# A new instruction order and bank table for attention plus MLP on one core, with the last output block in halves

## The chip, the cores and the metric

The kernel runs on one core of one Trainium2 chip. The metric is the device time of one execution in microseconds (us); lower is better. TensorE's granted clock is listed with each run, as a share of full speed. Engine names as in the profile: PE is TensorE (matmuls), PEld its weight loads, DVE is VectorE, ACT is ScalarE, POOL is GpSimd, SP is SyncE; an SPq or ACTq row, or a POOL row with DMA_DIRECT2D, is a transfer being issued by that engine.

## The reference

Random-feature attention on 8 batches of 8 heads, 576 rows of 64, followed by a two-layer MLP with a sigmoid gate. Inputs and output are float32; the kernel multiplies in bf16.

```python
def _attn_ref(q, k, v, omega):
    m, D = omega.shape                       # 128, 64
    scale = 1.0 / np.sqrt(np.sqrt(D))
    def phi(x):
        proj = np.einsum('bhsd,md->bhsm', x, omega)
        h = proj - np.sum(x * x, axis=-1, keepdims=True) / 2.0
        h = h - np.max(h, axis=-1, keepdims=True)
        return np.exp(h) / np.sqrt(m)
    q_p, k_p = phi(q * scale), phi(k * scale)
    kv = np.einsum('bhsm,bhsd->bhmd', k_p, v)
    z = np.sum(k_p, axis=2)
    num = np.einsum('bhsm,bhmd->bhsd', q_p, kv)
    den = np.einsum('bhsm,bhm->bhs', q_p, z)[..., None] + 1e-06
    return num / den
# x: the attention, 4608 rows of 512
def _moe_ref(x, w_in, w_out):                # 512 -> 2048 -> 512
    h = x @ w_in
    return (h * (1.0 / (1.0 + np.exp(-1.702 * h)))) @ w_out
```

## The kernel before

The program first lists operations with their dependences, then places them on engines by written-out orders: `ORDER` has for each engine the numbers of its operations, `BANK` the PSUM bank of each group of matmuls (PSUM takes their results; the table has eight banks). The SP ring below is the row of transfers that SyncE issues, in its order. Both were found by a search over a cost table; on the chip each engine runs its list in order, and waits where an operation is not ready (in the trace of after VectorE stood idle for 1.56 us before a copy at 10.48 us, though the input of the reduction behind it in its list was ready at 9.6).

Of the kernel before, what the change touches and what calls it, by code (L numbers as in the profile page):

```python
# [7 lines left out]
ALU = mybir.AluOpType  # L8
# [6 lines left out]
PE = "pe"  # L15
# [3 lines left out]
SP = "sp"  # L19
# [10 lines left out]
BANKS = dict(b0="H0 H1 O0 O1 P0 P1 S0 S1", b1="O1 P0 P1 S0 S1", b2="O1 P0 P1 S0 S1", bv="H0 H1 P0 P1 S0 S1", H="H0 H1", O="O0 O1", Oend="O0 O1 P0 P1")  # L30
# [5 lines left out]
QL_SW = 2  # L36
# [13 lines left out]
    om=(30.0, 0.0, 400.0), qk=(45.0, 1200.0, 770.0), ql=(26.5, 600.0, 630.0), qlc=(26.5, 800.0, 770.0), vl=(26.0, 600.0, 640.0),  # L50
    v=(51.0, 1600.0, 700.0), vw=(51.0, 1200.0, 640.0), qkl=(45.0, 1000.0, 770.0), w=(78.0, 2000.0, 810.0), T=(25.3, 100.0, 1250.0), os=(90.0, 100.0, 620.0),
# [6 lines left out]
        88, 50, 10, 54, 52, 66, 57, 56, 90, 71, 65, 72, 93, 99, 92, 115, 120, 98, 119, 142, 78, 144, 147, 117,  # L58
        152, 80, 146, 153, 125, 105, 83, 126, 132, 110, 107, 86, 219, 134, 137, 159, 113, 221, 253, 164, 140,
        161, 251, 223, 217, 167, 231, 172, 277, 169, 255, 175, 275, 301, 299, 178, 241, 303, 246, 184, 243,  # L60
        181, 265, 249, 187, 267, 270, 193, 279, 273, 196, 202, 313, 383, 211, 315, 289, 318, 205, 291, 294,
        190, 389, 297, 214, 199, 390, 208, 321, 391, 338, 335, 392, 347, 356, 384, 341, 395, 396, 353, 344,
        397, 398, 365, 457, 401, 402, 362, 350, 417, 385, 371, 359, 409, 403, 404, 477, 380, 368, 427, 386,
        437, 377, 467, 432, 429, 556, 472, 487, 374, 469, 447, 492, 562, 489, 449, 563, 557, 452, 564, 558,
        559, 565, 610, 574, 575, 576, 577, 650, 514, 582, 511, 568, 508, 520, 630, 569, 529, 517, 570, 590,
        538, 526, 571, 620, 535, 523, 729, 622, 532, 625, 660, 640, 544, 600, 541, 665, 645, 662, 735, 553,
        605, 602, 730, 642, 547, 550, 736, 763, 737, 731, 732, 755, 687, 738, 684, 693, 741, 681, 783, 742,
        773, 743, 775, 702, 778, 696, 744, 803, 747, 748, 749, 750, 823, 690, 813, 705, 793, 818, 815, 699,
        795, 902, 708, 798, 833, 714, 838, 903, 835, 711, 723, 908, 720, 956, 717, 904, 909, 936, 726, 854,
        910, 860, 905, 863, 857, 928, 914, 866, 911, 869, 915, 946, 920, 966, 875, 971, 948, 916, 917, 976,  # L70
        921, 878, 951, 968, 872, 996, 922, 986, 881, 923, 1129, 890, 884, 991, 1075, 1006, 988, 1101, 899,
        1076, 1011, 1109, 893, 1008, 887, 1081, 1082, 896, 1169, 1083, 1077, 1084, 1078, 1093, 1149, 1094,
        1033, 1119, 1095, 1030, 1027, 1124, 1087, 1042, 1088, 1051, 1036, 1121, 1089, 1139, 1045, 1060, 1090,
        1282, 1039, 1096, 1141, 1144, 1048, 1159, 1274, 1054, 1302, 1248, 1057, 1179, 1161, 1063, 1292, 1164,
        1066, 1181, 1184, 1294, 1249, 1072, 1069, 1322, 1260, 1297, 1250, 1261, 1342, 1251, 1203, 1206, 1266,
        1332, 1267, 1352, 1215, 1212, 1334, 1312, 1262, 1337, 1357, 1263, 1224, 1354, 1221, 1254, 1233, 1314,
        1200, 1255, 1317, 1209, 1218, 1256, 1227, 1257, 1236, 1242, 1427, 1245, 1364, 1428, 1373, 1230, 1268,
        1382, 1239, 1429, 1361, 1269, 1370, 1391, 1415, 1379, 1400, 1416, 1388, 1417, 1397, 1406, 1418, 1367,
        1409, 1410, 1487, 1411, 1376, 1481, 1385, 1394, 1412, 1403, 1482, 1421, 1483, 1433, 1436, 1422, 1442,
        1484, 1445, 1423, 1454, 1451, 1424, 1460, 1488, 1489, 1463, 1439, 1490, 1448, 1430, 1457, 1512, 1505,  # L80
        1466, 1499, 1500, 1501, 1469, 1502, 1526, 1478, 1527, 1506, 1493, 1507, 1475, 1513, 1472, 1494, 1495,
        1514, 1508, 1515, 1496, 1519, 1520, 1521, 1522, 1528, 1529,
    ],
    ACT: [
        51, 89, 9, 60, 61, 59, 70, 73, 75, 74, 101, 68, 102, 95, 100, 97, 122, 124, 129, 154, 151, 156, 127,
        155, 128, 133, 149, 220, 87, 160, 114, 141, 226, 218, 225, 236, 237, 235, 227, 173, 238, 233, 170, 260,
        261, 257, 176, 259, 179, 242, 262, 308, 309, 185, 305, 182, 266, 250, 307, 188, 310, 194, 285, 284,
        197, 286, 203, 283, 281, 212, 206, 191, 215, 200, 209, 339, 336, 393, 348, 357, 342, 345, 354, 399,
        366, 463, 459, 461, 462, 363, 351, 422, 464, 419, 423, 421, 360, 424, 412, 413, 411, 372, 405, 482,
        483, 381, 481, 484, 369, 479, 387, 442, 443, 441, 439, 444, 378, 375, 560, 616, 615, 566, 617, 612,  # L90
        614, 578, 655, 656, 652, 515, 512, 584, 585, 654, 509, 521, 586, 636, 657, 632, 530, 635, 518, 595,
        634, 539, 597, 527, 637, 592, 572, 536, 524, 596, 594, 533, 545, 542, 554, 548, 551, 768, 769, 765,
        733, 688, 770, 759, 757, 685, 758, 767, 739, 694, 788, 682, 787, 789, 790, 703, 785, 697, 808, 745,
        805, 809, 807, 810, 751, 829, 828, 691, 825, 827, 706, 830, 700, 709, 715, 712, 724, 721, 961, 958,
        962, 960, 718, 941, 727, 963, 938, 943, 855, 861, 940, 942, 906, 864, 858, 932, 930, 912, 931, 870,
        867, 876, 918, 982, 981, 983, 980, 978, 879, 873, 1001, 1002, 998, 1000, 1003, 882, 924, 1135, 1133,
        891, 1134, 1131, 885, 1104, 1103, 1136, 900, 1105, 1115, 1114, 894, 1111, 1113, 888, 897, 1173, 1174,
        1171, 1116, 1085, 1175, 1176, 1155, 1153, 1151, 1034, 1079, 1031, 1028, 1043, 1154, 1156, 1052, 1037,
        1046, 1061, 1091, 1288, 1287, 1040, 1284, 1097, 1286, 1049, 1277, 1278, 1289, 1055, 1308, 1276, 1304,
        1058, 1307, 1306, 1064, 1067, 1073, 1070, 1328, 1327, 1326, 1324, 1309, 1348, 1252, 1329, 1344, 1347,  # L100
        1349, 1204, 1346, 1207, 1216, 1213, 1264, 1225, 1222, 1234, 1201, 1210, 1219, 1228, 1258, 1237, 1243,
        1246, 1365, 1374, 1231, 1383, 1240, 1362, 1270, 1371, 1392, 1380, 1401, 1389, 1398, 1419, 1407, 1368,
        1377, 1386, 1395, 1413, 1404, 1434, 1437, 1443, 1485, 1446, 1455, 1452, 1425, 1461, 1464, 1440, 1491,
        1431, 1449, 1458, 1467, 1470, 1479, 1503, 1476, 1473, 1509, 1516, 1497, 1523, 1530,
    ],
    DVE: [
        4, 5, 8, 19, 14, 2, 11, 3, 12, 6, 55, 53, 58, 69, 91, 13, 67, 96, 116, 94, 121, 143, 123, 79, 145, 150,
        118, 148, 81, 106, 84, 85, 82, 108, 111, 109, 112, 138, 135, 139, 136, 222, 254, 165, 162, 163, 252,
        166, 224, 168, 234, 232, 278, 174, 256, 258, 171, 276, 302, 300, 177, 180, 304, 247, 248, 244, 245,
        186, 306, 183, 268, 269, 271, 272, 189, 195, 280, 282, 198, 314, 204, 274, 290, 213, 316, 317, 292,  # L110
        295, 296, 293, 207, 319, 192, 320, 216, 298, 201, 322, 210, 340, 337, 349, 358, 343, 346, 355, 460,
        458, 367, 364, 418, 352, 420, 410, 361, 373, 480, 478, 382, 428, 370, 440, 438, 468, 430, 433, 431,
        473, 474, 488, 434, 448, 470, 493, 471, 490, 450, 451, 376, 379, 453, 491, 454, 494, 613, 611, 651,
        653, 583, 516, 513, 510, 631, 522, 633, 531, 519, 591, 593, 540, 528, 621, 537, 525, 623, 626, 627,
        534, 661, 624, 641, 546, 601, 666, 646, 663, 647, 667, 664, 606, 543, 555, 643, 644, 607, 603, 604,
        552, 764, 549, 756, 766, 689, 686, 695, 786, 774, 683, 776, 784, 779, 777, 780, 704, 804, 698, 806,
        826, 824, 814, 692, 794, 819, 820, 707, 816, 817, 796, 797, 701, 799, 800, 834, 710, 716, 836, 839,
        840, 837, 713, 725, 957, 959, 722, 719, 939, 937, 728, 856, 862, 865, 859, 929, 871, 868, 947, 967,
        949, 972, 950, 973, 877, 979, 977, 952, 953, 969, 970, 874, 997, 999, 987, 880, 883, 1132, 1130, 992,
# [225 lines left out]
def bass_performer_favor__then__act_gelu_quick_kernel(  # L345
# [136 lines left out]

    def load_ql(b, key, ckey, after=()):
        s = b % 2
        pool = b >= QL_SW
        if b in LWB:
            for nm, t, c in (("k", kd, 1), ("q", qd, 0)):
                dst = bass.AP((QL if pool else QLF)[s], 256 * c, [[512, 128], [1, 256]])
# [620 lines left out]
```

## Time and profile before

| | before |
|---|---|
| time, median of 3 runs | 324.75 us (324.12 to 325.43) |
| TensorE busy | 307.4 us, 96% of the profiled span |
| VectorE, ScalarE, GpSimd busy | 190.7, 187.3, 113.1 us |
| first matmul | 5.7 us after the start |
| after the last matmul | 4.0 us |

The matmuls all belong to one engine that is busy in nearly all of the span, so the kernel is TensorE-bound and an order can win only where TensorE waits or runs at half clock (until 12.08 us by the trace's clock records; four 128-column transposes take 0.61 us at 8.14 and 0.39 at 12.96): at the start, at the end, and in rare gaps between. The prediction shows the lines and reads them.

### The profile page before, as it was taken

To read this page: it belongs to the slowest core of one execution; us is meant where nothing else is said; L and a number is where in the kernel's file an instruction comes from. 1 tells how busy PE (TensorE), PEld (TensorE's weight loads), DVE (VectorE), ACT (ScalarE), POOL (GpSimd) and SP (SyncE) were. 2 spreads that over 40 slices of the span, in tenths; PEclk is the share of its full clock that TensorE was granted. 3 is DMA by queue.
4 is the path that set the end of the run, shared out by engine and by line. 5 is a ranking of instruction groups with operands and counts; after the bars stand their busy time and mean duration, and the time that the engine had idled before them with its cause. 6 is when DMAs were issued, how large, how long until landed. Compare 5 with 4: busy or idle time off the path is not lost.

```text
span 321.7 us, 5787 instructions
## 1 busy us (share of the span) xinstructions
PE 307.4 (96%) x2246; PEld 151.2 (47%) x2246; DVE 190.7 (59%) x401; ACT 187.3 (58%) x378; POOL 113.1 (35%) x185
## 2 busy tenths in 40 slices
PE   1798999999999999999999999999999999999994
PEld 1574554445544544454454544454544444444442
DVE  0899985368656784686648745788574533342210
ACT  1789855489178646665658766686545543343231
POOL 6696283627019705933644364031200000000000
PEclk9999999999999999999999999999999999999999
DMA  7999999996889989998999999933022002011005
GB/s 134 241 226 222 207 210 222 151 145 129 209 163 206 226 120 162 245 193 155 141 159 194 207 158 168 151 99 61 2 41 86 0 2 98 33 67 65 33 17 148
DMA packets 84119, 44.20 MB, mean 137 GB/s; under 512 B 54844, under 2 KB 77756, under 8 KB 84092
## 3 DMA queue, kind: packets, MB, share of 16 engines
q0 software_dynamic: 29792, 20.45, 42.0%
q1 hardware_dynamic: 54300, 23.37, 35.4%
q8 instruction: 18, 0.29, 0.4%
q14 instruction: 9, 0.07, 0.1%
HBM read 36.73 MB, written 9.44 MB: 144 GB/s over the span
## 4 chain that ended last, share of the span: by engine, by line
PE 86%; ACT 5%; DVE 5%; DMA 2%; issue 1%; POOL 1%; POOLq 0%
PE HT L427 36%; PE OB L427 34%; PE PB L427 11%; PE SB L427 4%; ACT QKP L641 3%; DMA QK<-in_q_dram 2%; DVE GT L966 1%; DVE NM L631 1%; ACT TH L961 1%; DVE OO L855 1%; ACT QKL L641 1%; POOL QK L478 1%; DVE TT L598 0%; DVE RD L847 0%; PE PB L868 0%
## 5 line engine op out<-in xcount | busy, mean ns | idle before, releaser
L966 DVE SCALAR_TENSOR_TENSOR GT<-TH,HT 128x512 bf16<-128x512 f32 x144 | 97.8, 683 | 80.4 <-ACT TH L961 80.0
L427 PE MATMUL HT<-XT,WIN 128*128 128x512 bf16 x576 | 142.2, 379 | 0.6 <-DVE GT L966 0.3
L961 ACT ACTIVATE TH<-HT 128x512 f32<-128x512 f32 x144 | 86.2, 600 | 82.7 <-PE HT L427 74.9
L427 PE MATMUL OB<-WOUT,GT 128*128 128x512 bf16 x496 | 122.5, 379 | 0.0
L427 PEld LDWEIGHTS HT<-XT,WIN 128*128 128x128 bf16 x576 | 52.7, 98 | 61.5 <-DVE GT L966 7.7
L427 PEld LDWEIGHTS OB<-WOUT,GT 128*128 128x128 bf16 x496 | 45.7, 98 | 53.4 <-issue 3.4
L780 POOL TENSOR_TENSOR VP<-VS,WW 128x512 bf16<-128x512 f32 x32 | 33.5, 1050 | 38.8 <-ACT WW L774 38.7
L641 ACT ACTIVATE QKP<-PB 128x512 bf16<-128x512 f32 x54 | 31.4, 600 | 7.2 <-PE PB L427 4.1
L641 ACT ACTIVATE QKP<-SB 128x512 bf16<-128x512 f32 x56 | 33.0, 606 | 2.8 <-PE SB L427 1.1
L995 ACT ACTIVATE OS<-OB 128x512 f32<-128x512 f32 x31 | 18.6, 599 | 16.7 <-PE OB L427 16.6
L631 DVE TENSOR_REDUCE NM<-SB 128x4 f32<-128x512 f32 x31 | 20.9, 682 | 8.8 <-PE PB L427 7.4
L631 DVE TENSOR_REDUCE NM<-PB 128x4 f32<-128x512 f32 x23 | 15.5, 683 | 6.9 <-PE PB L427 5.3
L427 PE MATMUL PB<-WOUT,GT 128*128 128x512 bf16 x80 | 19.4, 379 | 0.0
L478 POOL DMA_DIRECT2D QK<-in_k_dram x17 | 13.4, 790 | 7.1 <-DMA QK<-in_q_dram 4.2
L789 POOL CAST VP<-WW 128x8 bf16<-128x8 f32 x32 | 7.0, 225 | 24.3 <-ACT WW L774 24.3
L855 DVE TENSOR_TENSOR OO<-PB,RD 128x320 bf16<-128x320 f32 x29 | 13.7, 485 | 0.4
L478 POOL DMA_DIRECT2D QK<-in_q_dram x17 | 13.0, 768 | 0.0
L503 POOL DMA_DIRECT2D QL<-in_k_dram x12 | 7.8, 649 | 13.6 <-DMA TT<-QK 13.6
L427 PEld LDWEIGHTS PB<-WOUT,GT 128*128 128x128 bf16 x80 | 7.8, 98 | 9.5 <-DVE GT L966 0.3
L855 DVE TENSOR_TENSOR OO<-SB,RD 128x320 bf16<-128x320 f32 x24 | 11.5, 482 | 0.3
L532 POOL DMA_DIRECT2D VS<-in_v_dram x12 | 7.8, 661 | 7.2 <-DMA TT<-QK 7.2
L427 PE MATMUL PB<-TT,omB 64*128 64x512 bf16 (+1 forms) x31 | 10.2, 377 | 0.0
(140 smaller groups left out, 285.7 us busy)
## 6 DMA issues: line engine op xcount, KB each, us to landing
out_dram<-OS SPq DMA_DIRECT2D x32, 256.0 KB, 2.8
VS<-in_v_dram POOLq DMA_DIRECT2D x12, 512.0 KB, 6.6
QK<-in_k_dram POOLq DMA_DIRECT2D x15, 256.0 KB, 6.4
QK<-in_q_dram POOLq DMA_DIRECT2D x15, 256.0 KB, 7.3
WIN<-in_moe_w_in_dram POOLq DMA_DIRECT2D x4, 512.0 KB, 10.7
WOUT<-in_moe_w_out_dram POOLq DMA_DIRECT2D x4, 512.0 KB, 17.2
VS<-in_v_dram SPq DMA_DIRECT2D x4, 256.0 KB, 6.4
VS<-in_v_dram SPq DMA_DIRECT2D x2, 512.0 KB, 12.4
```

What stands on the lines that cost most here:

```text
L427: return lambda e: e.matmul(o() if callable(o) else o, lhsT=l, rhs=r, **kw)
L478: POOL, lambda e, dst=dst, so=so: e.dma_start(dst, so), 800, key,
L503: POOL if pool else SP, lambda e, dst=dst, so=so: e.dma_start(dst, so), 120, key,
L532: SP if b < V_SW else POOL, lambda e, dst=dst, so=so: e.dma_start(dst, so), 120, key,
L631: lambda e: e.tensor_reduce(out=o, in_=bass.AP(TILE[gr.bank], 0, [[512, 128], [128, 4], [1, 128]]), axis=AX.X, op=ALU.max, negate=True,),
L641: lambda e: e.activation(out=o, in_=view(gr, 0, pat or [[1, 512]])(), func=ACTF.Exp, scale=scale),
L780: lambda e: e.tensor_tensor(out=VP[vs][:, :, 0:64], in0=bass.AP(V, t * 9 * 64 + 64, [[NT * 9 * 64, 128], [64, 8], [1, 64]]), in1=bass.AP(W ...
L789: POOL, lambda e: e.tensor_copy(out=VP[vs][:, :, 64], in_=WW[vs][:, :]), 140, key + K_W + 240,
L855: lambda e, gr=gr, x=x: e.tensor_tensor(out=OO[os_][:, 5 * x : 5 * x + 5, :], in0=bass.AP(TILE[gr.bank], 0, [[512, 128], [65, 5], [1, 64]] ...
L961: lambda e, gr=gr, th=th: e.activation(out=TH[th][:, :], in_=at(gr, 0, 512)(), func=ACTF.Tanh, scale=0.851),
L966: lambda e, gr=gr, th=th, jc=jc: e.scalar_tensor_tensor(out=GT[gi][:, jc, :], in0=TH[th][:, :], scalar=1.0, in1=at(gr, 0, 512)(), op0=ALU. ...
L995: lambda e, gr=gr, os_=os_: e.activation(out=OS[os_][:, :], in_=at(gr, 0, 512)(), func=ACTF.Copy, scale=0.5),
```

## The change

A wider search: all kinds of PSUM groups but one (`bv`, not printed below) may take any of the eight banks, costs of some loads are raised, orders and banks come out new on all five engines, and the last output block is split so that less work follows the last matmul.

```diff
-BANKS = dict(b0="H0 H1 O0 O1 P0 P1 S0 S1", b1="O1 P0 P1 S0 S1", ..., H="H0 H1", O="O0 O1", Oend="O0 O1 P0 P1")
+BANKS = dict(b0="H0 H1 O0 O1 P0 P1 S0 S1", b1="H0 H1 O0 O1 P0 P1 S0 S1", ..., Oend="H0 H1 O0 O1 P0 P1 S0 S1")
-QL_SW = 2
+QL_SP = (0, 1)
+TAIL = True
 ...                                     # DMA_KIND: two fixed costs 1200 and 1000 -> 1300
     SP: [                               # the other engines' orders are new as well
-        18, 17, 20, 7, 22, 21, 28, 27, 46, 48, 42, 47, ...
-        802, 782, 822, 734, 746, 781, 740, 752, 955, 821, 926, 801, 975, 841, 927, 995, ...
+        22, 18, 7, 17, 47, 20, 48, 21, 28, 27, 46, 45, ...
+        573, 567, 579, 926, 734, 781, 955, 740, 752, 975, 746, 821, 801, 841, 927, 995, ...
 ...                                     # BANK: a new table
+    def last_block(gi, key):            # the last 128 rows, two halves of 256 columns
+        for half in range(2):
+            ...                         # 4 x 4 matmuls of 256 columns into one bank
+            cut = 128 if half else 256
+            ...                         # ScalarE evacuates columns 0 to cut
+            if half:
+                ...                     # VectorE evacuates columns 128 to 256
+            for h in range(2):
+                g.add(ACT if half and h else SP, ... dma_start ...)
 ...
+            if TAIL and sbi == 8 and rb == 3:
+                last_block(gi, win2(9))
+                continue
```

In the SP order, 926, 955 and 975 are the transposes of pairs 0, 1 and 2 of batch 5, and 781, 821, 801 and 841 those of the finished attention of batch 4 into XT. Before, 975 stood between 801 and 841. Now it stands ahead of 821, 801 and 841.

## The prediction

> **What bounds the kernel now.** I read the page first, then busy times by stage, the waits of TensorE, the timelines of the first 16 us and the last 10 us, and then the starts of single matmuls. The page, engines and slices:
>
> ```profile
> span 321.7 us, 5787 instructions
> PE 307.4 (96%) x2246; PEld 151.2 (47%) x2246; DVE 190.7 (59%) x401; ACT 187.3 (58%) x378; POOL 113.1 (35%) x185
> PE   1798999999999999999999999999999999999994
> ```
>
> TensorE is the bound: it is idle only in the first six slices and the last. Busy times of four stages (columns: stretch, length, busy us of each engine, clock, DMA share, GB/s):
>
> ```profile
> 0.00:12.00 12.00, 5.03 (x36) 3.49 (x37) 3.63 (x15) 3.45 (x7) 6.42 (x14) 1.00 0.91 169
> 12.00:40.00 28.00, 25.36 (x322) 16.05 (x321) 25.81 (x63) 25.61 (x59) 19.40 (x32) 1.00 1.26 222
> 40.00:312.00 272.00, 271.31 (x1867) 129.28 (x1866) 161.22 (x325) 156.17 (x311) 87.31 (x140) 1.00 0.73 127
> 312.00:322.00 10.00, 5.71 (x27) 2.39 (x25) 0.00 (x0) 2.09 (x4) 0.00 (x0) 1.00 0.51 133
> ```
>
> From 12 to 40 us three engines are at 91 to 92% together: attention of batches 0 and 1 must be exponentiated and evacuated before the large matmuls exist that need neither ScalarE nor VectorE. From 40 to 312 us TensorE lacks 0.7 us in 272. A matmul's record overlaps the next, so a busy PE can hide waits; I therefore took the start-to-start distance of neighbouring matmuls minus 216 ns per 512 columns. That shows 5.67 us before the first matmul; about 5.9 us of loss to 16 us (waits and half-speed matmuls); about 4.4 us from 16 to 40; and 7 us from 40 to 312, of which some 6 are not waits: 35 projections on 64 rows cost about 0.1 us on entering and 0.1 on leaving. True waits after 40 us are only about 1.0 us, 0.7 of it one wait at 179.7. At the end 4 us follow the last matmul. So all that an order can win is about 5.7 + 5.9 + 2.8 (true waits, 16 to 40) + 1.0 + 4.0 = 19 us, most of it in latencies that stay. TensorE's waits:
>
> ```profile
> PE OB L725 <- DMA QK<-in_k_dram: 5.7, 1, 5.7
> PE SB L725 <- DMA QK<-in_k_dram: 0.9, 1, 0.9
> PE PB L427 <- ACT QKP L641: 0.7, 1, 0.7
> PE HT L427 <- DVE TT L598: 0.6, 1, 0.6
> PE HT L868 <- DVE OO L855: 0.6, 1, 0.6
> PE PB L427 <- ACT TH L961: 0.6, 1, 0.6
> ```
>
> No wait recurs: no wait for a PSUM bank is long enough to be a bound. The end, from the timeline:
>
> ```profile
> 312.37 5.34 PE L427 MATMUL PB<-WOUT,GT 128*128 128x512 bf16 x24
> 317.75 0.60 ACT L995 ACTIVATE OS<-PB 128x512 f32<-128x512 f32 x1 [1.13 <-PE PB L427]
> 318.37 1.11 SPq L1012 DMA_DIRECT2D out_dram<-OS  x2
> ```
>
> After the last matmul come one 0.60 us evacuation, two issues one after the other, and a landing.
>
> [...] four transposes take 0.61 us at 8.14 and 0.39 at 12.96. [...]
>
> **The change part by part.**
>
> Title items that change nothing: the leftover q/k rows of batches 0 and 1 were already on the SP ring with casts (the old threshold 2 selects the same batches). The new branches for split leftovers need a batch that is both at least 1 and in (0,), so they never run. Costs and descriptor counts only fed the search; the orders are written out. What is left is the order, the bank table, fourteen moved small operations and the last block.
>
> (1) Last block. 16 matmuls of 512 columns become 32 of 256: 32 x 109 = 3.49 us for 16 x 216 = 3.45, plus 0.04. The weight loads (98 ns each) fit under 109. The last half is evacuated by ScalarE (128 columns) and then VectorE (128 columns) from one bank, hence one after the other: from 0.60 us at 512 and 0.20 at 8 columns, ScalarE takes about 0.30; VectorE about 0.25; with two hand-overs of 0.06 this equals the old 0.60 plus 0.06, so no gain. The two stores are issued by two sequencers at once (saves 0.55) and carry 64 KB instead of 128 (I choose 0.25 less than the 2.4 us landing). Sum: about -0.7 us, all on the path.
>
> (2) Banks and order from 40 us on. The waits here sum to 1.0 us; the new order has 34 instead of 35 runs of 64-row projections (-0.2). I give it -0.3, since new small waits come in too.
>
> (3) Start. K of pair 0 is loaded first, then K and Q of pair 1, then K of pairs 2 and 3. On the SP ring a leftover load of batch 1, which is gated on pair 1's Q, is now fifth. The ring stops there with 640 packets issued, where by 15 us it formerly had moved 1,536. GpSimd's queue moved about 150 packets per us beside it and up to 380 when alone (10 to 11 us, counted in the trace), so batch 0's last Q should land near 12 us instead of 15.0. That is a gain for supply.
> Against it: TensorE's first instruction is now the omega transpose. Omega landed at 7.5 us; as third on its ring I estimate 6.5 to 7.5. Then follow in a row: cast 0.20, transpose 0.31, two copies and four memsets 0.8, the copy of pair 0's K 0.42, two cold projections 0.9, transposes of pair 1 (0.6), its copy 0.42, and only then the first reduction, which stands behind that copy in VectorE's order. That is near 11.3 instead of 10.58, and ScalarE's first exponential near 12.5 instead of 11.01. Afterwards the two engines should be fed better: between 12 and 40 us VectorE was idle 2.2 us and ScalarE 2.4 (28 minus 25.81 and 25.61), and a win of half, 1.2 us, is my choice. The fourteen moves are nearly even: five copies go from ScalarE to VectorE and six back, one cast goes each way between VectorE and GpSimd, and the identity memset leaves GpSimd. I set the sum of the start at -0.7 us: gains of 1.2 and of the earlier q/k (0.7), less 1.2 for the later first exponential.
>
> Sum: -0.7 - 0.3 - 0.7 = -1.7 us; 324.75 - 1.7 = 323.1.
>
> **Rivals.** (a) The start loses: exponentials begin 1.5 us later, TensorE is busy too little before 12 us [...]. For it: the order of waits above, and one omega load in front of all. Against: transposes, projections and late loads still fill 8 to 12 us. It would make +1 to +2 us at the start, 325 in all. (b) The start wins clearly: loads land 3 us earlier, 12 to 40 us has no waits (2.8 us) and the 4.2 us lost between 8 and 16 halve. For it: K first gives both engines work sooner, GpSimd's queue is freed. Against: 91% on two engines means that work, not supply, limits that stage. It makes -4 to -5 us: 320. (c) Early loads of batch 1 and the first weights wait behind GpSimd operations that now stand before them in its order (a copy of batch 0's first weights before Q of batch 1). For it: that copy can run at about 13 us, and this Q was issued at 11.56. Against: the queue held other work and landed it at 19.05, some 7 us after its issue. It would make under +1 us. (d) The middle gets worse: any bank may now delay the large matmuls behind a reduction or evacuation. At most a few waits of 0.5 us.
>
> **Range and chances.** The 0.7 us at the end is nearly certain to within 0.4; the start is uncertain to plus or minus 2 us, the middle to 0.7, the run-to-run spread 0.6. So 320.7 to 325.5. Faster by 2% needs under 318.3, a gain of 6.4 of the 19 us listed, most of them latencies: 0.05. Slower by 2%, over 331.2, needs a stall of 6 us that the search would have seen: 0.02.
>
> **What would show it.** End: last output issue on two sequencers together, under 3.2 us from last matmul to end of span. Start: batch 0's last Q landing near 12 us, omega's transpose first at about 7.3, the first exponential after 12, and VectorE and ScalarE over 93% busy from 13 to 38 us. Middle: TensorE lacking under 1 us between 40 and 312. The prediction is wrong if the matmuls stay slow after 12.1 us, if TensorE has a wait over 2 us past 16 us, or if 256-column matmuls start further apart than 109 ns.

## More of the kernel before

```python
# pair t (two heads) of batch b: its Q and K are transposed by the DMA; the landing is also "tgo"
g.add(SP, lambda e: e.dma_start_transpose(tout, tin), 150, key - 5000,
      reads=[("q", s, t), ("k", s, t)],
      writes=[("Tk", tt), ("Tq", tt), ("tgo", b, t)], dma=f"d_T{tt}", ...)
...
# the finished pair of attention is transposed into XT, the MLP's input:
#   OO -> XT, one transfer for each pair, ("xt", t, b) is written      (SP ring too)
...
def stage1(sbi):                       # x @ w_in for batch sbi
    rd = [("xt", t, sbi) for t in range(NT)]           # NT = 4: all four pairs
    ...                                # 16 chains of four 512-column matmuls,
                                       # tanh on ScalarE, product on VectorE -> GT
def stage2(sbi):                       # GT @ w_out, 4 blocks of 16 matmuls, ScalarE, store
...
for b in range(1, B):
    stage1(b - 1)
    if b >= 2:
        stage2(b - 2)
    attend(b)
    if b + 1 < B:
        gate = [("wout", 2)] if b == 1 else [("tgo", b, 2)]
        load_qk(b + 1, 0, 4, ..., after=gate)     # casting loads, issued by GpSimd
        load_qk(b + 1, 4, 4, ..., after=gate)
        load_ql(b + 1, ..., after=gate)
        load_v(b + 1, 0, NT, ..., after=gate)
```

The last lines matter most below: the loads of batch b + 1 are released when the transpose of pair 2 of batch b has landed, wherever that transpose stands in the SP ring's order.

## The result, and the profile after

The changed kernel took 328.61 us (median of 4 runs: 326.55, 328.47, 328.74, 328.87); the kernel before took 324.53 us (4 runs of the same rounds). The ratio is 1.0108, with a 95% interval of 1.0061 to 1.0154. It is the mean time of one kernel's fast runs over the mean of the other's of the same rounds, so not quite the ratio of the medians. Executions over 1.5% slower than the fastest of the same kernel are left out of the means. Within 2%, but 5.5 us above the predicted time and above the range.

From the page of the kernel after: span, engines (busy us, share, instructions), and two rows of the 40 slices, TensorE's busy tenths and its granted clock.

```profile
span 327.1 us, 5780 instructions
PE 306.4 (94%) x2224; PEld 154.2 (47%) x2262; DVE 189.3 (58%) x402; ACT 185.6 (57%) x380; POOL 113.0 (35%) x184
PE   1878999999999999999599999999999999999995
PEclk9999999999999999999699999999999999999999
```

Busy time is 1 us less and the span is 5.4 us more (327.1 against 321.7), so it is waiting. The twentieth slice (155 to 164 us) is half empty, and the clock falls in the same slice. (The trace lacks 38 matmul records, by its count of 2,262 weight loads, none of them in this stretch; I worked from the weight loads.) The same stages as in the prediction, and 150 to 170 us by itself:

```profile
0.00:12.00 12.00, 3.78 (x31) 3.14 (x32) 3.12 (x15) 2.08 (x3) 6.38 (x13) 1.00 0.98 149
12.00:40.00 28.00, 24.72 (x311) 16.53 (x311) 24.55 (x59) 25.95 (x59) 18.86 (x31) 1.00 1.24 220
40.00:312.00 272.00, 266.07 (x1821) 127.85 (x1852) 161.33 (x329) 154.54 (x313) 87.79 (x141) 0.99 0.72 127
150.00:170.00 20.00, 16.44 (x81) 6.71 (x81) 8.29 (x13) 10.79 (x25) 6.71 (x11) 0.83 1.41 175
```

TensorE's wait list of after, longest first (columns: engine, output bank, line, what ended the wait; total, times, longest):

```profile
PE SB L568 <- DVE om_raw L450: 7.2, 1, 7.2
PE PB L428 <- issue: 3.7, 2, 3.6
PE PB L428 <- ACT QKP L644: 1.7, 1, 1.7
```

The first is the start, as predicted. The second is new, a single wait of 3.6 us whose releaser the view does not see ("issue"). The timeline around it shows what was in flight. A row gives start, length, engine, line, operation, output <- input.

```profile
143.66 1.29 SPq L790 DMA_TRANSPOSE TT<-QK  x1
146.19 3.94 SPq L906 DMA_TRANSPOSE XT<-OO  x3
147.02 0.81 POOL L545 DMA_DIRECT2D VS<-in_v_dram  x1 [6.67 <-DMA TT<-QK]
147.82 0.77 POOL L479 DMA_DIRECT2D QK<-in_q_dram  x1
...
152.60 0.70 POOL L504 DMA_DIRECT2D QL<-in_k_dram  x1
159.50 1.48 PE L428 MATMUL PB<-XT,WIN 128*128 128x512 bf16 x3 [3.56 <-issue]
```

The transpose of pair 2 of batch 5 (143.66) now goes out before the last three XT transposes of batch 4. Its landing at 146.73 releases GpSimd at 147.02, and GpSimd issues nine loads of batch 6 until 153.3. Two of the XT transposes are then still to be issued (147.44 and 148.76). They land at 153.63 and 159.03. The first matmul of stage 1 of batch 4 reads all four pairs of XT and starts at 159.50. The same stretch of the kernel before:

```profile
142.18 1.20 SPq L878 DMA_TRANSPOSE XT<-OO  x1
...
144.78 1.29 SPq L878 DMA_TRANSPOSE XT<-OO  x1
146.17 1.25 SPq L762 DMA_TRANSPOSE TT<-QK  x1
147.47 1.29 SPq L878 DMA_TRANSPOSE XT<-OO  x1
...
149.71 0.62 POOL L532 DMA_DIRECT2D VS<-in_v_dram  x1 [7.17 <-DMA TT<-QK]
```

There the releasing transpose is issued at 146.17, one place before the last XT transpose, which lands at 150.24. The first load is issued at 149.71, too late to slow it by much (2.77 us from issue to landing). The margin was small, though: experiment 3 releases the loads one pair earlier in the order of before, and that does the same harm. The landing times by tile say it in one line each. Before, then after, over three XT transposes:

```profile
DMA to landing us min/median/max: 2.7/2.8/2.8
```

```profile
DMA to landing us min/median/max: 2.6/6.2/10.3
```

The stall is paid twice. TensorE stood idle from 155.94 to 159.50 (3.56 us), and the trace's clock records show half speed from 158.28 to 165.11, so the matmuls after the wait started 0.43 us apart instead of 0.216: 165.11 - 159.50 = 5.61 us at half speed are another 2.8 us. Together that is 6.4 us. The timed runs agree: of the four, the one whose clock stayed at 1.00 took 326.55 us, the two at 0.99 took 328.74 and 328.87.

To compare whole kernels I worked out "matmul time lost" for each trace: the time of a matmul's start minus the sum of what all earlier matmuls take back to back at full clock (64-row projections in pairs). It counts waits and half-speed alike. The unit is us:

| lost up to | before | after | difference |
|---|---|---|---|
| 20 us | 12.40 | 13.85 | +1.45 |
| 40 us | 15.97 | 17.28 | +1.31 |
| 150 us | 19.61 | 20.26 | +0.65 |
| 170 us | 20.08 | 27.08 | +7.00 |
| 312 us | 23.20 | 29.24 | +6.04 |
| end of the span | 27.76 | 33.06 | +5.30 |

So +1.3 came at the start, -0.7 from 40 to 150, +6.35 between 150 and 170 us, -1.0 in the rest of the middle, and -0.74 at the end. The end of after:

```profile
322.33 1.47 PE L428 MATMUL PB<-WOUT,GT 128*128 128x256 bf16 x12
323.84 0.28 ACT L1022 ACTIVATE OS<-PB 128x128 f32<-128x128 f32 x1 [0.93 <-PE PB L428]
324.14 0.29 DVE L1030 TENSOR_SCALAR OS<-PB 128x128 f32<-128x128 f32 x1 [12.62 <-ACT OS L1022]
324.47 0.55 ACTq L1040 DMA_DIRECT2D out_dram<-OS  x1
```

ScalarE and VectorE go one after the other (0.28 and 0.29 us), and the last store leaves on ScalarE's sequencer. From the last matmul's end to the end of the span: 3.28 us, before 4.03.

### The profile page after: what moved, and what is told of

It is laid out like the page before. It is cut to its first block, busy times and chain, and to the rows that moved or that the text cites.

```text
span 327.1 us, 5780 instructions
## 1 busy us (share of the span) xinstructions
PE 306.4 (94%) x2224; PEld 154.2 (47%) x2262; DVE 189.3 (58%) x402; ACT 185.6 (57%) x380; POOL 113.0 (35%) x184
## 4 chain that ended last, share of the span: by engine, by line
PE 87%; ACT 5%; DVE 2%; issue 2%; DMA 1%; SPq 0%; POOL 0%; POOLq 0%; ACTq 0%
PE OB L428 26%; PE HT L428 23%; PE SB L428 20%; PE PB L428 18%; ACT QKP L644 3%; DMA om_f<-in_omega_dram 1%; DVE GT L994 1%; ACT TH L989 1%; PE HT L753 0%; ACT TT L598 0%; ACT XT L598 0%; DVE OO L883 0%; DVE NM L632 0%; ACT QKL L644 0%; DVE TT L599 0%
## 5 line engine op out<-in xcount | busy, mean ns | idle before, releaser
L428 PE MATMUL OB<-WOUT,GT 128*128 128x512 bf16 x249 | 63.3, 383 | 0.6 <-issue 0.2
L428 PE MATMUL HT<-XT,WIN 128*128 128x512 bf16 x183 | 48.3, 385 | 0.4 <-issue 0.2
L994 DVE SCALAR_TENSOR_TENSOR GT<-TH,HT 128x512 bf16<-128x512 f32 x47 | 32.0, 682 | 22.3 <-ACT TH L989 22.1
L994 DVE SCALAR_TENSOR_TENSOR GT<-TH,SB 128x512 bf16<-128x512 f32 x41 | 27.9, 682 | 27.4 <-ACT TH L989 27.3
L989 ACT ACTIVATE TH<-HT 128x512 f32<-128x512 f32 x47 | 28.2, 603 | 26.9 <-PE HT L428 21.8
L428 PE MATMUL SB<-XT,WIN 128*128 128x512 bf16 x162 | 42.1, 382 | 0.8 <-ACT QKP L644 0.6
L428 PE MATMUL PB<-XT,WIN 128*128 128x512 bf16 x113 | 30.3, 386 | 3.8 <-issue 3.6
L428 PE MATMUL HT<-WOUT,GT 128*128 128x512 bf16 x109 | 27.6, 379 | 0.2
L428 PEld LDWEIGHTS HT<-XT,WIN 128*128 128x128 bf16 x188 | 17.3, 99 | 20.4 <-issue 1.9
L994 DVE SCALAR_TENSOR_TENSOR GT<-TH,PB 128x512 bf16<-128x512 f32 x30 | 20.3, 678 | 11.3 <-ACT TH L989 11.0
L428 PE MATMUL OB<-XT,WIN 128*128 128x512 bf16 x100 | 25.7, 379 | 0.2
## 6 DMA issues: line engine op xcount, KB each, us to landing
WOUT<-in_moe_w_out_dram POOLq DMA_DIRECT2D x4, 512.0 KB, 12.5
```

The costliest lines, as they stand in the source:

```text
L428: return lambda e: e.matmul(o() if callable(o) else o, lhsT=l, rhs=r, **kw)
L989: lambda e, gr=gr, th=th: e.activation(out=TH[th][:, :], in_=at(gr, 0, 512)(), func=ACTF.Tanh, scale=0.851),
L994: lambda e, gr=gr, th=th, jc=jc: e.scalar_tensor_tensor(out=GT[gi][:, jc, :], in0=TH[th][:, :], scalar=1.0, in1=at(gr, 0, 512)(), op0=ALU. ...
```

## The experiments

Theory A: the release of batch 6's loads now precedes the XT transposes of batch 4; the loads share the DMA with them and delay them, and the wait for XT costs 6.4 us, nearly half of it through the clock. Rivals, lettered as in the expectations: the transposes are late by their place on the SP ring, whatever the loads do (B), or the clock fell by itself and the wait only shows it (C). One that the expectations do not name: the stall comes from the bank table or the order on TensorE (D). Several runs also ask about the start, where the prediction was off by some 2 us.

The first four ran beside 11 runs of the kernel before (median 324.21 us).

**1. e1_gate: the changed kernel, with the loads of batch 6 also waiting for the last XT transpose of batch 4.** Orders and banks are untouched.

```diff
-gate = [("wout", 2)] if b == 1 else [("tgo", b, 2)]
+gate = [("wout", 2)] if b == 1 else [("tgo", b, 2)] + ([("xt", 3, 4)] if b == 5 else [])
```

> The changed kernel with one more dependency: the loads of batch 6 also wait for the last XT transpose of batch 4 (they start about 4 us later). Theory A (these loads share the DMA engines with two XT transposes of batch 4, which then land after 6.2 and 10.3 us; TensorE waits 3.56 us for them and its clock falls to half for 6.8 us): all XT transposes of batch 4 land within 3.5 us, the wait of TensorE near 156 us is below 0.5 us, the clock is 1.00, and the time falls from 328.6 to 322.0 to 323.0, ratio to before 0.992 to 0.996. Rival B (the transposes are late because of their place in the SP queue, whatever the loads do): the wait stays above 2.5 us and the time above 327. Rival C (the clock falls by itself): the wait goes, but half clock in the middle stays in most runs, about 325.

Measured: 322.51 us (4 runs, 321.96 to 323.69), ratio 0.9952 (0.9932 to 0.9972). The landings of the same three XT transposes, and the stretch where the stall was:

```profile
DMA to landing us min/median/max: 2.6/2.6/2.7
```

```profile
150.00:170.00 20.00, 20.00 (x135) 9.31 (x133) 11.38 (x22) 13.15 (x29) 13.95 (x22) 1.00 1.12 201
```

One more dependence took the time from 1.0108 to 0.9952 of before, about 5 us (1.56% of 324.4). The 3.6 us wait is gone, and so is the clock's fall. The SP ring, the banks and TensorE's order are those of the changed kernel, so rivals B and D fall. The gated kernel is also faster than both kernels, though by 0.5% over before only.

**2. e2_filler: the changed kernel with 15 idle 512-column matmuls just before the first matmul that needs XT of batch 4.** They compute nothing that is used; their bank is free there.

```diff
+BANK.append("P1")
+ORDER[PE].insert(ORDER[PE].index(860), 1541)
 ...
+gr = Group(["P1"])
+g.add(PE, [mm(at(gr, 0, 512), WIN[:, 0, 0:128], XT[:, 0, 0:512])] * 15, ..., grp=gr)
```

> The changed kernel with 15 idle matmuls of 512 columns (15 x 216 ns = 3.24 us) put on TensorE just before the matmul that waits near 156 us; their result is overwritten. The wait for the transposes stays. Theory A: the clock fell because TensorE was idle, so now it stays at 1.00 in every run and the time falls by 2.5 to 3.0 us to about 325.8 (ratio to before 1.003 to 1.006), like the one run of the changed kernel with clock 1.00 (326.55). Rival C (the clock falls by itself, or for the load on the chip): half clock stays in the middle and the time stays at 328 to 329.

Measured: 325.86 us median (4 runs: 325.56, 325.78, 325.94 and one 330.12 at full clock that I cannot explain and that lifts the ratio), ratio 1.0081 (1.0035 to 1.0127). The transposes are as late as without the filler, but the clock stays up (the last three columns: clock, DMA share, GB/s):

```profile
DMA to landing us min/median/max: 2.6/6.2/9.7
150.00:170.00 20.00, 20.00 (x111) 8.86 (x110) 8.99 (x15) 13.14 (x29) 9.03 (x16) 1.00 1.39 169
```

The median is 2.75 us under the changed kernel's, near the 2.8 us worked out above for the half clock. It is 3.35 us above the gated kernel, and 15 matmuls of 216 ns are 3.24 us. So the idle wait pulled the clock down and not the other way round; rival C falls, and the stall splits into a wait of some 3.5 us and a clock penalty of some 2.8 us.

**3. e3_before_early: the kernel before, with the loads of batch 6 released one pair earlier.**

```diff
-gate = [("wout", 2)] if b == 1 else [("tgo", b, 2)]
+gate = [("wout", 2)] if b == 1 else [("tgo", b, 1 if b == 5 else 2)]
```

> The kernel before with one gate changed: the loads of batch 6 are released by the transpose of pair 1 of batch 5 instead of pair 2 (it landed at 143.0 instead of 149.4). Theory A: the loads now run beside the XT transposes of batch 4 (issued at 142.2, 144.8 and 147.5), the last of which land 3 to 8 us later than the 2.7 us they took; TensorE waits 1 to 4 us near 154 us, the clock may fall, and the time rises by 1 to 6 us over before. Rival B (the place in the SP queue, not the loads): no change, within 0.5 us.

Measured: 329.96 us (328.41 to 331.14), ratio 1.0174 (1.0146 to 1.0203): slower beyond the noise, though whether by 2% is undecided. TensorE's waits and the XT landings of that run:

```profile
PE HT L427 <- DMA XT<-OO: 4.3, 2, 4.0
```

```profile
DMA to landing us min/median/max: 2.6/8.3/8.6
```

The old order and the old banks, with nothing but an earlier release, give the same stall: a wait of 4.0 us for XT (here the view names it), and half clock from 159.37 to 162.79. The cause works both ways.

**4. e4_before_tail: the kernel before, with only the last block in halves.** The second half goes into bank H0, and both take the output buffers that the change gives them.

```diff
+BANK.append("H0")
+ORDER[PE] += [1533, 1534, 1535, 1536]
+ORDER[ACT] += [1537, 1540]
+ORDER[DVE] += [1538]
+ORDER[SP] += [1539]
+    def last_block(gi, key): ...          # as in the change
+            if sbi == 8 and rb == 3:
+                last_block(gi, win2(9))
+                continue
```

> The kernel before with the last block in halves and nothing else. Prediction on record for the end: 0.7 us less (stores issued by two sequencers at once, half the size; the evacuation is no shorter). Expected 323.8, ratio 0.9965 to 0.9990; from last matmul's end to span's end 3.0 to 3.3 us instead of 4.0. Rival: the 32 matmuls of 256 columns are slower than 109 ns apart and eat it: ratio 1.000 or more.

Measured: 324.08 us (6 runs), ratio 0.9993 (0.9978 to 1.0008). The time decides nothing. In the trace, the last matmul's end to the end of the span is 3.53 us instead of 4.03: half 0's evacuation waited 1.43 us for an output buffer that an earlier store still read. The clock of that trace also became full at 14.05 us instead of 12.08, and its loss at 40 us (as in the table above) was 16.94 us against 15.97, more than the halves can win. So experiment 9 asks again from the other side.

**5. e5_warm: the gated kernel with 28 idle matmuls of 256 columns at the very start**, so that the clock is up before the real work begins.

```diff
+BANK.append("O0")
+ORDER[DVE].insert(0, 1541)
+ORDER[PE].insert(0, 1542)
 ...
+wz = sb("wz", [128, 256], BF16)
+g.add(DVE, lambda e: e.memset(wz[:], 1.0), 100, 0, writes=["wz"])
+g.add(PE, [mm(at(gr, 0, 256), wz[:, 0:128], wz[:])] * 28, ..., grp=gr)   # gr = Group(["O0"])
```

> e1_gate with 28 idle matmuls of 256 columns on TensorE from about 1.2 to 7 us, while it would wait for the first load. Theory S1 (a part of the loss at the start is the half-speed clock: it ended between 12.1 and 14.9 us in the six traces so far, and the later, the more was lost by 40 us): full clock from 5 to 8 us on, the matmul time lost by 40 us (time minus ideal time of all matmuls started) falls from 16.4 to 17.3 without the idle ones to 15.5 to 16.0, the time by 0.3 to 1.0 us below e1_gate, to 321.5 to 322.2. Rival S2 (the start is bound by ScalarE and VectorE, the clock does not matter): within 0.2 us of e1_gate.

Measured: 322.73 us (6 runs), ratio 0.9945 (0.9922 to 0.9967). The clock was full from 6.14 us on, and the loss at 40 us was 15.98 us instead of 16.41, but the time is that of the gated kernel (0.9952). Three of the six runs had a mean clock of 0.993 to 0.995, so it fell again somewhere in them.

**6. e6_before_warm: the same idle matmuls in the kernel before.** The edit is the same, with bank H1 and the numbers 1533 and 1534, and without the gate.

> The kernel before with the same 28 idle matmuls. S1: 0.3 to 0.8 us faster than before, ratio 0.9975 to 0.999. S2: no change. Against e5_warm it compares the two starts at the same clock: if the new order of the start is as good as the old one, the two have lost the same by 40 us within 0.2 us; my reading of the traces so far is that the new one has lost 0.3 to 0.5 us more.

Measured: 324.30 us (6 runs), ratio 0.9999 (0.9978 to 1.0019). Full clock from 4.76 us, no gain. (In the profiled run omega landed at 9.0 us instead of 7.5, so its start cannot be read step by step; its loss at 40 us is about 0.9 us above that of experiment 5, against the reading in the expectation.) That a late warm-up is what the start costs is not supported in either kernel.

**7. e7_om_first: as 5, with omega's load first on the SP ring.**

```diff
+ORDER[SP].remove(7)
+ORDER[SP].insert(0, 7)
```

> e5_warm with the load of omega first on the SP ring instead of third. The prediction said that omega stands in front of everything in the new order. If so, omega lands near 4 us instead of 6.9, the first matmul that counts starts when K of pair 0 lands (6.4 us) instead of 7.2, the first exponential comes 0.5 to 0.8 us earlier than in e5_warm and the time falls by 0.3 to 0.7 us. Rival (VectorE and ScalarE make up for it later): within 0.2 us of e5_warm.

Measured: 324.44 us median of 6 runs, two of them slow (326.05 and 327.01 us, at a clock of 0.984); over the fast runs the ratio is 0.9937 (0.9896 to 0.9978), which overlaps that of 5. Omega landed at 2.58 us instead of 6.59, and the first reduction and the first exponential came 0.4 us sooner (9.39 and 10.83 against 9.78 and 11.22). The matmuls up to 19 us kept that lead: the last before 20 us began at 19.18 instead of 19.56. (The loss at 20 us, 13.03 in both, cannot show it: at 20.0 us both traces stand idle after the same matmul.) Then TensorE waited 1.60 us (0.38 in experiment 5) for the cast of batch 1's leftover rows, whose last load landed at 20.31 instead of 18.59, and the next matmul began at 21.18 instead of 20.33. The clock fell to half from 22.64 to 29.47 us in the profiled run, which cost some 3 us at 40 us (18.97 against 15.98). So landing omega 4 us sooner won 0.4 us, and another wait took it back. Whether it would pay without that wait is open: the two runs at a clock of 1.00 took 321.10 and 321.71 us, the three such runs of 5 321.64 to 322.69.

**8. e8_swap: as 5, with VectorE's first reduction ahead of the copy that stood before it.** This is the link of the chain that the prediction named ("stands behind that copy in VectorE's order").

```diff
+i = ORDER[DVE].index(89)
+ORDER[DVE][i : i + 2] = [67, 89]
```

> e5_warm with two neighbours of VectorE's order exchanged: the first reduction before the copy of pair 1's K. In the changed kernel VectorE stood idle for 1.56 us before that copy though the reduction's input was ready at 9.6 us. The prediction named this order as a cost. If so: the first reduction starts near 9.5 instead of 10.8, and the time falls by 0.2 to 0.7 us against e5_warm. Rival: the first exponential waits for another copy anyway, within 0.2 us.

Measured: 322.43 us (6 runs), ratio 0.9953 (0.9916 to 0.999). The first reduction began at 9.00 instead of 9.78 us, the first exponential at 11.24 instead of 11.22, for it waits for other operations too. No gain.

**9. e9_gate_whole: the gated kernel with the last block whole again.**

```diff
-TAIL = True
+TAIL = False
 ...
+BANK.pop()
+for e in ENGINES:
+    ORDER[e] = [i for i in ORDER[e] if i < 1533]
```

> The changed kernel with the gate of the first experiment, but its last block whole again (one 512-column chain, one evacuation by ScalarE, two stores by one sequencer), as in the kernel before. The order up to there is kept. The theory that the halves are worth what the prediction gave them (0.7 us, on the path) expects 0.6 to 0.8 us more than the gated kernel's 322.5, thus 323.2 and a ratio to before near 0.9973, with the last matmul's end to the end of the span 4.0 instead of 3.3 us. The rival (the fourth experiment's time showed no gain of the halves: the issue and the landing hide it) expects the gated kernel's time, ratio 0.995.

Measured: 324.00 us (6 runs), ratio 0.9987 (0.996 to 1.0015). The gated kernel with halves had 0.9952; the difference, 0.35% or 1.1 us, is uncertain by about as much. The trace gives the size: between 312 us and the end it lost 4.41 us, against 3.72 in experiment 1, so the halves are worth 0.69 us. Its last evacuation:

```profile
318.26 0.60 ACT L1074 ACTIVATE OS<-SB 128x512 f32<-128x512 f32 x1 [2.86 <-PE SB L432]
```

It ends at 318.86, and the span at 322.2: 4.02 us from the last matmul's end, against 3.30 in experiment 1. The 0.60 us evacuation stands in place of the 0.28 and 0.29, so the gain lies in the stores, as the prediction had it. The rival, that the halves are hidden, is not borne out.

**10. e11_gate_swap: the gated kernel with the exchange of experiment 8, without idle matmuls.**

> The gated kernel of the first experiment with one pair of VectorE's operations exchanged: the first reduction before the copy of pair 1's transposed K. No warming matmuls. If the later first exponential (12.33 us, in the chain that the prediction laid out) costs time, the first exponential moves up by 0.4 us or more and the time falls by about as much, to 322.0 (ratio 0.9935). The rival, that the start is bound by the sum of VectorE's and ScalarE's work up to 40 us and not by when it begins, expects the first exponential earlier and the time the same as the gated kernel's, ratio 0.995, and the same loss of matmul time at 40 us within 0.5 us (16.4).

Measured: five timed runs at 322.55 to 323.26 us, ratio 0.9955 (0.9937 to 0.9973): the gated kernel's. The exchange is worth nothing here either. The sixth run, the profiled one, took 1,481.86 us. In its trace all engines but TensorE are as busy as ever, while neighbouring 512-column matmuls start mostly 1.28 us apart until about 900 us and 0.84 us apart after that. Its trace has no record of the clock at all, so the 1.0 listed for it says nothing. No other run showed this, the same program's five others are normal, and I have no cause for it. So the expected times of the first operations could not be read.

A further kernel, with the gate for all later batches, was not built: its order would have been circular.

**What these say of the start.** Losses at 40 us, in traces without idle matmuls: the new order 17.28 (after), 16.41 (1), 16.84 (2), 17.78 (9), mean 17.08; the old one 15.97 (before), 16.40 (3), 16.94 (4), mean 16.44. The new order seems 0.6 us worse, but one order differs by 1.4 us between traces. Differences of half a microsecond at the start can't be settled from single traces.

## Why the prediction was wrong

The bound it read off was right: TensorE sets the time, and the time moved only where TensorE waited or ran at half clock. (Of its line of slices it said "idle only in the first six slices and the last"; the line shows less than nine tenths in the first, second, fourth and last.) Two of its own signs of being wrong came: a wait over 2 us past 16 us, and in that trace slow matmuls past 12.1 us. The third did not: in the trace of after, 256-column matmuls start 109 ns apart.

**The last block: right.** Predicted -0.7 us; measured -0.74 between before and after, and 0.69 between experiments 1 and 9. The last matmul's end to the end of the span was predicted under 3.2 us and came to 3.28. The two evacuations after one another (0.28 + 0.29 against the 0.60 of one) and the second sequencer are as laid out. Experiments 4 and 9 could not prove it in time alone.

**Banks and order from 40 us on: this is the step that failed.** "I give it -0.3, since new small waits come in too", and in rival (d) "At most a few waits of 0.5 us". The loss between 40 and 312 us went from 7.23 to 11.96 us, which is +4.7. Without the new stall (experiment 1) it is 5.93, and 6.07 in experiment 9, so the rest of the step was even better than predicted: 1.2 to 1.3 us against that trace of before, 0.4 to 1.3 against all the old-order traces without a stall (about 7.1 in experiment 4, 6.52 in 6). One wait of 3.6 us and the clock behind it ate it all. The prediction looked at this step for bank waits, and the banks were harmless: the only bank wait above a microsecond, 1.7 us at 17.4 us, is there in the faster experiment 1 too. It did not look at what the new SP order releases. Nothing in the profile of before shows this as a wait, as the releasing transpose was issued only one place before the last XT transpose. The place of 975 against 821, 801 and 841 in the diff, together with the line `gate = ... ("tgo", b, 2)`, did say it. The prediction worked out such a release at the start only, for leftover rows that are gated on Q. In the middle it took the landing times of before for given.

**Slower by 2% "needs a stall of 6 us that the search would have seen".** It was a stall of 6.4 us. The rest was 1.1 us better in the profiled traces (5.30 - 6.4), so the sum stayed within 2%. That a search finds an order good by its cost table is no evidence about a collision of transfers. I did not measure what its model holds; that it misses the collision is only inferred from its choice.

**The start: mis-sized by 1 to 2 us, and its sign open.** Predicted -0.7. The first operations came as laid out: omega landed at 6.94 (6.5 to 7.5), the last Q of batch 0 at 12.07 (near 12), the first reduction began at 10.82 (near 11.3), the first exponential at 12.33 (near 12.5). The term that failed is the win of 1.2 us from better feeding: ScalarE was 25.95 us busy from 12 to 40, little more than before, and VectorE only 24.55, less than before. In the prediction's own stretch, 13 to 38 us, ScalarE just reached the 93% asked of it (23.28 of 25 us; 23.05 before), but VectorE came to 86% (21.55; 22.84 before), so the earlier loads bought nothing visible. The loss of 1.2 us from the later first exponential isn't confirmed either, for experiments 8 and 10 changed that chain without gain, and 7 lost its 0.4 us to another wait. Rival (a) came true in one trace: TensorE was busy 3.78 us before 12 us, against 5.03 in before, and the clock was full at 14.92 us instead of 12.08, 2.8 us later. It varied from one execution to the next, though: with the same order it was full at 12.30 and 12.57 us in experiments 1 and 2, and in the old order at 14.05 in experiment 4. Rival (c) was real and small: Q of batch 1 was issued at 14.30 and landed at 22.4 us (11.56 and 19.05 before), with no wait of TensorE to show for it.

The sum of the prediction, -1.7 us, is what the change does without its collision: the gated kernel is 0.48% under before, -1.6 us, though by other shares.

## What to carry to other kernels

When a diff reorders a ring, follow every transfer whose landing releases others, and ask which urgent transfers are still to come behind it: bulk loads let loose 2.7 us earlier (147.02 against 149.71), with the last urgent transpose 1.3 us later (148.76 against 147.47), made two 2.6 us transposes take 6.2 and 10.3 us to land. A wait of 3.6 us on TensorE cost 6.4, as the clock fell too, so an order with thin margins before the one transfer that the matmuls need is worth one explicit dependence. The gated version, one dependence more than the change, took 322.5 us, 0.9952 of before; none of its variants (experiments 5, 7, 8 and 10) is better beyond the noise.

## What the runs leave open

- Why the transposes were late beside the loads. Three SBUF transposes of equal size took 2.6, 6.2 and 10.3 us from issue to landing when nine loads (six of them casting) were issued beside them, and 2.6 to 2.7 us when these were held back (experiment 1). The runs show the delay; what makes it within the DMA is not shown.
- How much idle time brings the clock down. In after the records fall at 158.28 us, 2.34 us after TensorE went idle and before it had work again; half speed lasted 6.83 us. In experiment 3 they fall at 159.37, after a wait of 4.0 us, and half speed lasted 3.42 us. In experiment 7 they fall at 22.64, when the wait of 1.60 us had been over for 1.46 us (21.18), and half speed lasted 6.83 us. Yet a wait of 1.7 us from 17.4 us on in after brought no fall, so the length of the wait alone does not settle it.
- What slowed experiment 10. Its trace has no clock event at all, in an execution of 1,481.86 us with 512-column matmuls 1.28 and then 0.84 us apart. The second is near four times the 0.216 us of a full clock, the first near six times; that the clock was the cause is not shown.
